# One fused retention and feed-forward kernel: the hand-written step table up to block 2, in another order

## The chip, the cores and the metric

The kernel runs on one core of one Trainium2 chip. The measure is device time in microseconds of one execution, of which lower is better. Six engines matter here: TensorE (PE, with its weight loads shown as PEld), VectorE (DVE), ScalarE (ACT), GpSimd (POOL), SyncE (SP), and the DMA engines, whose transfers are issued by SP, POOL and, at the start and the end, ACT. Each engine carries out its own instructions in the order in which they stand in the program; between engines only semaphores set an order.

## The reference: what is computed

Two layers, one after the other. The first is a retention layer (attention without softmax, with a decay per head) on q, k, v of 8 batches, 8 heads, 576 positions and 64 channels:

```
scores = (q @ k^T) / sqrt(64)
ret    = scores * gamma[h] ** (i - j)      for j <= i, else 0
x      = ret @ v                           heads side by side: 4608 tokens x 512
```

The second is a feed-forward layer on the 4608 tokens, with a snake activation, w_in of 512 x 2048, w_out of 2048 x 512 and one alpha for each of the 2048 columns:

```
h   = x @ w_in
g   = h + sin(alpha * h) ** 2 / (alpha + 1e-9)
out = g @ w_out
```

Inputs and output are float32; the kernel computes in float16 with float32 sums.

## The kernel before, in words

**Blocks.** The 512 first positions of each of the 8 batches make blocks 0 to 7 of 512 tokens; the 64 last positions of all batches make block 8. A block's x must be there before its feed-forward part, so attention for batch n+1 is done beside the feed-forward part of block n.

**Attention of one batch.** k and q come in halves of 256 positions (p = 0, 1), are scaled by powers of the decay and cast to float16 (step C, line 215, or line 210 on ACT), and are transposed, on PE for batches 0 and 1 and the first half of batch 2 (TR, copied out of PSUM by TK) or by a transposing DMA (CR). SP gives scores in PSUM, SM multiplies them by the causal mask (line 393; SO first copies them to float16), OU sums k times v over chunks of 128 positions, and FS, FA, NS and TS carry the state from chunk to chunk (FA and NS on two engines in turn: fade, then add; TS writes the state in float16, line 346). VA (line 462) adds masked scores times v to the output bank, ST (line 488) adds q times the state; XT copies the finished x to SBUF.

**Feed-forward part of one block.** GEMM1 has 16 units of four 512-column matmuls (line 584; G1 or H1 in the table). Each unit is followed by a sine on ACT (SI, line 593), a square (SQ, on ACT line 602, on DVE or POOL line 604) and a product that adds h (PR, on DVE, line 609), which writes gT and frees the PSUM bank. For the first four pairs of units of block 0 this is done in half blocks of 256 tokens (H1, HS, HQ, HP; lines 1067, 1079, 1094). GEMM2 has for each of four groups of 128 tokens four parts of four matmuls (line 623); part r reads gT of units 4r to 4r+3. The finished group is copied out of PSUM (line 633, or step OS) and stored by SP.

**What sets the order.** The steps up to block 2's start stand in a table, TABLE, one line a step, and the engine is often its last letter (V, A, G). follow() carries out the table line by line; as the scheduling is manual, an engine's queue holds its instructions in that order. Step LV n p loads v (POOL's queue), WI g and WO g load a quarter of w_in and w_out (POOL's queue), LK b nm p loads half of q or k (SP's queue; a last word names a load that it waits for), KB n m issues n filler matmuls of m columns, which write a PSUM bank that nobody reads. Behind the table a loop over blocks 2 to 8 takes over: each turn does one GEMM1 unit, then what todo lists for that unit (attention of the next batch at units 0, 4, 8 or so), the square, the product and one GEMM2 part from a list, `second`, which holds the parts of blocks 1 to 8 in order. Step GN in the table takes one part from the same list ahead of the loop. Where a part is the last of its group (`last`), the square and the product come after it:

```
second = [(n, u) for n in range(1, NBLK) for u in range(12 if n == NBLK - 1 else 16)]
...
    last = second[0][1] % 4 == 3
    if not last:
        square(n, u, A_); product(n, u)
    next_second()
    if last:
        square(n, u, A_); product(n, u)
while second:
    next_second()
```

What is still in the list after the loop is done at the end, followed by the last group in two halves (line 1228).

PSUM banks come from three pools: hp (three banks), op (one) and mm (two pairs); a step that takes a bank waits until the last reader of its former use is done. Raw q and k share six buffers.

Of the kernel before, what the change touches and what calls it, by code (L numbers as in the profile page):

```python
# [16 lines left out]
def kernel(  # L17
# [630 lines left out]
TR 0 0 k 1  # L648
LV 0 0
TR 0 0 q 1  # L650
KB 2 512 op
LV 0 1
WI 0
LK 0 k 1
LA
NO 0 0
TK 0 0 q AV
TK 0 0 k AV
SP 0 0 1
SP 0 0 0  # L660
AL
SO 0 0 0
AC
LP 0 q 1 0
LP 0 q 1 1
C 0 k 1 0 G
KB 2 512 op
C 0 k 1 1 G
TR 0 1 k 1
KB 2 512 hp  # L670
TK 0 1 k AA
C 0 q 1 1 G
WI 1
# [7 lines left out]
VA 0 0 1  # L681
FS 0
FA 0 0 V 1
TS 0 0 V
ST 0 0
NS 0 1
FA 0 1 G
OU 0 1 1
TS 0 1 V
NS 0 2  # L690
TS 0 2 G
AO
WI 2
TK 0 1 q AA
SP 0 1 0
SM 0 1 0
XT 0 0 AA
SP 0 1 1
SM 0 1 1
H1 0 1 0 op  # L700
HS 0 1 0
H1 0 0 0 hp
FA 0 2 G
NS 0 3
HS 0 0 0
HQ 0 0 0 V
HP 0 0 0
HQ 0 1 0 G
ST 0 1
VA 0 1 1  # L710
VA 0 1 0
H1 0 2 0 hp
XT 0 1 A
WO 0
WO 1
LK 1 q 0 w_in2
LK 1 k 0
LK 1 q 1 w_in2
LK 1 k 1 w_in2
HP 0 1 0  # L720
H1 0 3 0 mm
H1 0 0 1 mm
# [2 lines left out]
HP 0 2 0  # L725
HS 0 3 0
HQ 0 3 0 V
TS 0 3 G
HS 0 0 1
HQ 0 0 1 A  # L730
H1 0 1 1 op
H1 0 2 1 hp
H1 0 3 1 hp
G1 0 8 hp
HP 0 0 1
HP 0 3 0
# [12 lines left out]
HQ 0 2 1 G
HP 0 2 1  # L750
SQ 0 8 G
PR 0 8
HP 0 3 1
SQ 0 9 G
SQ 0 10 A
PR 0 10
PR 0 9
G1 0 12 hp
SI 0 11
SI 0 12  # L760
# [11 lines left out]
SQ 0 15 A  # L772
SQ 0 14 G
PR 0 13
C 1 q 0 1 V
PR 0 15
G2 0 0 0 op
G2 0 0 1 op
LV 1 0
G2 0 1 0 hp  # L780
G2 0 3 0 hp
G2 0 1 1 hp
PR 0 14
LV 1 1
C 1 q 0 0 G
WO 2
LK 2 q 0 w_out2
C 1 k 0 0 A
C 1 k 0 1 A
TR 1 0 q  # L790
LV 2 0
TR 1 0 k
G2 0 2 0 hp
TK 1 0 k A
LK 2 k 0 w_in0
LK 2 k 1 w_in1
LK 2 q 1 w_in1
C 1 k 1 1 V
TK 1 0 q V
SP 1 0 1  # L800
SP 1 0 0
G2 0 3 1 hp
SO 1 0 1
C 1 k 1 0 V
SO 1 0 0
C 1 q 1 1 G
C 1 q 1 0 G
# [5 lines left out]
G2 0 2 1 hp
TK 1 1 k A
SP 1 1 0
SM 1 0 1
OU 1 0
# [35 lines left out]
C 2 k 0 1 V
FA 1 2 G
NS 1 3
C 2 q 0 0 V
# [97 lines left out]
VA 2 1 0
SI 1 13
C 3 k 1 0 G
SQ 1 13 A
PR 1 13
PR 1 10
G1 1 14 hp  # L960
# [12 lines left out]
PR 1 15
C 3 q 1 0 G
LV 3 0
TS 2 3 G
CR 3 1
GN 1
"""

    HALVES = [(0, "k"), (0, "q"), (1, "k"), (1, "q")]
# [1 line left out]
    V, A_, G_ = nc.vector, nc.scalar, nc.gpsimd  # L983

    with tc.manual_schedule():
# [174 lines left out]
        for n in range(2, NBLK):  # L1160
            A = A2
# [104 lines left out]
```

## Time and profile before

| | |
|---|---|
| time, median of 3 runs | 308.93 us (308.0 to 310.65) |
| the profiled execution's own time | 308.69 us |
| its span, first to last instruction | 306.7 us |
| TensorE busy | 296.4 us, 97% of the span |
| ScalarE busy | 227.0 us, 74% |
| VectorE busy | 191.6 us, 62% |
| GpSimd busy | 135.2 us, 44% |
| HBM read and written | 36.91 MB and 9.44 MB |
| granted TensorE clock | 1.00 |

The profile is of one execution; its own time is 2 us more than its span, for what lies before the first and behind the last instruction. Timelines list for each row the start, the time that the row spans, engine, line, operation, what is written and read, shapes and count; in brackets stands how long the engine was idle before and what ended that. A single 512-column matmul is shown with 0.38 us since its end is modelled, but such matmuls start 0.216 us after one another; four of them (a unit or a part) take 0.865 us of TensorE.

### The profile page before, as it was taken

How to read it: one execution, taken by the hardware profiler on the slowest of the kernel's cores; microseconds unless marked ns; L12 is line 12 of the kernel's file. 1: busy time of each engine (PE TensorE's matmuls, PEld its weight loads, DVE VectorE, ACT ScalarE, POOL GpSimd, SP SyncE). 2: the span in 40 equal slices, each digit the busy share in tenths (PEclk: the TensorE clock that was granted, in tenths of full speed). 3: DMA queues.
4: the chain of work that ended last, by engine and by line, in shares of the span. 5: the costliest groups of instructions: out<-in, count | busy, mean ns of one | idle time of the engine just before them, and what ended most of it. 6: DMA issues, size and time to landing. Idle time of an engine off the chain costs nothing.

```text
span 306.7 us, 7628 instructions
## 1 busy us (share of the span) xinstructions
PE 296.4 (97%) x3134; PEld 152.8 (50%) x3134; DVE 191.6 (62%) x266; ACT 227.0 (74%) x378; POOL 135.2 (44%) x158
## 2 busy tenths in 40 slices
PE   8789999999999999999999999999999999999994
PEld 7476445544444444544454445544544444444444
DVE  2878958799565357946997699546665333444401
ACT  1579873999688887788778878787877888888810
POOL 3887664869949839703960297219000000000000
PEclk9999999999999999999999999999999999999999
DMA  7999999997999787999899989984331111122133
GB/s 212 218 195 204 262 185 246 248 250 128 167 177 227 129 210 183 155 177 221 175 161 196 172 214 165 151 138 76 71 68 37 35 34 36 36 54 47 36 68 68
DMA packets 118017, 44.74 MB, mean 146 GB/s; under 512 B 84432, under 2 KB 113504, under 8 KB 117984
## 3 DMA queue, kind: packets, MB, share of 16 engines
q1 hardware_dynamic: 83792, 35.08, 56.5%
q0 software_dynamic: 33600, 8.92, 30.0%
q8 instruction: 24, 0.39, 0.5%
q10 hardware_dynamic: 592, 0.28, 0.4%
q14 instruction: 9, 0.07, 0.1%
HBM read 36.91 MB, written 9.44 MB: 151 GB/s over the span
## 4 chain that ended last, share of the span: by engine, by line
PE 79%; DMA 6%; DVE 5%; POOL 5%; ACT 2%; issue 2%; POOLq 0%; DVEq 0%; ACTq 0%
PE ops L623 36%; PE hps L584 33%; DMA w_in<-in_moe_w_in_dram 3%; DMA w_out<-in_moe_w_out_dram 3%; DVE gT L609 2%; PE o L462 2%; PE o L488 2%; PE hps L1067 2%; POOL v L128 1%; POOL q L215 1%; PE ops L1228 1%; DVE ret L393 1%; POOL ss_t L604 1%; ACT s_t L593 1%; PE kv L312 1%
## 5 line engine op out<-in xcount | busy, mean ns | idle before, releaser
L609 DVE SCALAR_TENSOR_TENSOR gT<-ss_t,inva,hps 128x512 f16<-128x512 f16 x136 | 100.4, 744 | 80.3 <-ACT ss_t L602 79.9
L623 PE MATMUL ops<-w_out,gT 128*128 128x512 f16 x560 | 140.9, 379 | 0.5 <-DMA w_out<-in_moe_w_out_dram 0.5
L584 PE MATMUL hps<-x,w_in 128*128 128x512 f16 x480 | 120.9, 379 | 1.0 <-DVE gT L609 0.6
L593 ACT ACTIVATE s_t<-hps,alpha_t 128x512 f16<-128x512 f32 x136 | 92.9, 685 | 33.1 <-PE hps L584 31.7
L584 PEld LDWEIGHTS <-w_in 128*128 128x128 f16 x544 | 53.0, 98 | 64.5 <-issue 1.6
L623 PEld LDWEIGHTS <-gT 128*128 128x128 f16 x560 | 53.0, 98 | 61.2 <-issue 0.7
L602 ACT ACTIVATE ss_t<-s_t 128x512 f16<-128x512 f16 x127 | 79.9, 631 | 2.7
L346 POOL TENSOR_TENSOR s<-kvs,cn 128x512 f16<-128x512 f32 x28 | 30.6, 1093 | 57.0 <-ACT kvs L319 50.1
L633 ACT COPY osb<-ops 128x512 f32<-128x512 f32 x31 | 18.2, 586 | 11.7 <-PE ops L623 11.7
L126 POOL DMA_DIRECT2D v<-in_v_dram x32 | 22.0, 728 | 0.0
L393 DVE TENSOR_TENSOR ret<-sc,mask 128x1024 f16<-128x1024 f32 x12 | 14.4, 1215 | 4.6 <-PE sc L376 4.6
L215 DVE TENSOR_TENSOR q<-q,cn 128x512 f16<-128x512 f32 x17 | 14.1, 854 | 4.3 <-DMA q<-in_q_dram 4.3
L584 PE MATMUL hps<-x_rest,w_in 128*128 128x512 f16 x64 | 16.4, 379 | 0.0
L215 POOL TENSOR_TENSOR q<-q,cn 128x512 f16<-128x512 f32 x14 | 15.5, 1120 | 0.1
L432 DVE TENSOR_TENSOR ret<-sc,two 128x1024 f16<-128x1024 f32 x12 | 14.6, 1218 | 0.0
L604 POOL TENSOR_TENSOR ss_t<-s_t 128x512 f16<-128x512 f16 x10 | 10.5, 1059 | 6.6 <-ACT s_t L593 5.0
L236 ACT CAST x<-o 128x1024 f16<-128x1024 f32 (+1 forms) x13 | 10.8, 851 | 3.1 <-PE o L488 2.7
L359 POOL TENSOR_TENSOR kvs<-s,kvs 128x256 f32<-128x256 f32 x15 | 11.5, 769 | 1.2
L358 POOL TENSOR_TENSOR s<-kvs,cn 128x256 f32<-128x256 f32 x15 | 11.0, 731 | 0.0
L462 PE MATMUL o<-ret,v 64*64 64x128 f16 (+1 forms) x512 | 9.4, 213 | 0.6 <-DVE ret L393 0.6
L215 POOL TENSOR_TENSOR k<-k,cn 128x512 f16<-128x512 f32 x9 | 9.9, 1106 | 0.4 <-DMA k<-in_k_dram 0.4
L215 DVE TENSOR_TENSOR k<-k,ct 128x512 f16<-128x512 f32 x12 | 10.0, 830 | 0.0
(74 smaller groups left out, 209.0 us busy)
## 6 DMA issues: line engine op xcount, KB each, us to landing
out_dram<-osb SPq DMA_DIRECT2D x70, 128.0 KB, 3.3
q<-in_q_dram SPq DMA_DIRECT2D x14, 512.0 KB, 7.5
k<-in_k_dram SPq DMA_DIRECT2D x32, 128.0 KB, 5.1
k<-in_k_dram SPq DMA_DIRECT2D x7, 512.0 KB, 7.1
q<-in_q_dram SPq DMA_DIRECT2D x8, 256.0 KB, 5.3
v<-in_v_dram POOLq DMA_DIRECT2D x8, 256.0 KB, 6.0
w_in<-in_moe_w_in_dram POOLq DMA_DIRECT2D x4, 512.0 KB, 8.1
w_out<-in_moe_w_out_dram POOLq DMA_DIRECT2D x4, 512.0 KB, 7.8
```

The costliest lines, as they stand in the source:

```text
L126: nc.gpsimd.dma_start(t_[halves(g), :, s], v[b, :, xs, :].rearrange("h i d -> i h d"))
L215: eng.tensor_tensor(half[b, nm, p][:, :, :, t, :], raw[b, nm, p].rearrange("p (a t) (r d) -> p a t r d", t=2, r=2)[:, :, t], (ct if nm == ...
L346: (eng or nc.gpsimd).tensor_tensor(d_, self.kvs[:, n].unsqueeze(2).to_broadcast([P, 4, 2, D]), g2.unsqueeze(3).to_broadcast([P, 4, 2, D]), ...
L393: nc.vector.tensor_tensor(ret.rearrange("p t (z x) -> p (t z) x", z=2)[:, :, 0:n], sc.rearrange("p t (z x) -> p (t z) x", z=2)[:, :, 0:n], ...
L432: nc.vector.tensor_tensor(ret.rearrange("p t (a x) -> p (t a) x", a=n), sc.rearrange("p t (a x) -> p (t a) x", a=n), m_.unsqueeze(1).to_br ...
L462: nc.tensor.matmul(o[g][halves(t), x0 : x0 + 128].rearrange("p (r i) -> p r i", r=2)[:, :, i0:], x, y, start=(t, g) not in begun, stop=las ...
L584: nc.tensor.matmul(hps, w_in16[:, a, fc * P : (fc + 1) * P], x_of[n][:, a], start=(a == 0), stop=(a == KT - 1),)
L593: nc.scalar.activation(s_t, hps, mybir.ActivationFunctionType.Sin, bias=0.0, scale=alpha_t[:, fc : fc + 1],)
L602: nc.scalar.activation(ss_t, s_t, mybir.ActivationFunctionType.Square)
L609: nc.vector.scalar_tensor_tensor(gT[n][:, fc, :], ss_t, inva[:, fc : fc + 1], hps, MULT, ADD)
L623: nc.tensor.matmul(ops[n, c], gT[n][:, fk, c * P : (c + 1) * P], w_out16[:, fk, :], start=(fk == 0), stop=(fk == FC - 1),)
L633: nc.scalar.copy(osb, ops.pop((n, c)))
```

## The change

Only TABLE is altered. It has one line less: of the three places with fillers between the first transposes and the first H1 (`KB 2` each) one is left, with `KB 3`; and a third GN has been added, so that three parts of block 1's GEMM2 stand ahead of the loop instead of two. All other lines are the same steps in another order, some on another engine. Line numbers behind the table are lower by one in the changed kernel. The diff, cut to what moves a wait, a load or an engine:

```diff
 TR 0 0 q 1
-KB 2 512 op
 LV 0 1
 WI 0
 LK 0 k 1
 LA
+LP 0 q 1 0
 NO 0 0
 TK 0 0 q AV
+LP 0 q 1 1
+C 0 k 1 1 G
+C 0 k 1 0 G
 TK 0 0 k AV
 SP 0 0 1
 SP 0 0 0
 AL
+KB 3 512 hp
+AC
 SO 0 0 0
-AC
-LP 0 q 1 0
-LP 0 q 1 1
-C 0 k 1 0 G
-KB 2 512 op
-C 0 k 1 1 G
 TR 0 1 k 1
-KB 2 512 hp
...
 FA 0 0 V 1
+NS 0 1
 TS 0 0 V
 ST 0 0
-NS 0 1
...
-TS 0 2 G
+WI 2
 AO
-WI 2
...
-FA 0 2 G
+FA 0 2 V
 NS 0 3
 HS 0 0 0
-HQ 0 0 0 V
+HQ 0 0 0 A
 HP 0 0 0
-HQ 0 1 0 G
+TS 0 2 G
...
+WO 1
 WO 0
-WO 1
+HQ 0 1 0 G
+TS 0 3 G
 LK 1 q 0 w_in2
-LK 1 k 0
+LK 1 k 0 w_in2
 LK 1 q 1 w_in2
-LK 1 k 1 w_in2
+LK 1 k 1 w_out1
...
 G1 0 11 op
+SI 0 11
 HQ 0 2 1 G
 HP 0 2 1
 SQ 0 8 G
-PR 0 8
 HP 0 3 1
 SQ 0 9 G
+PR 0 9
+PR 0 8
 SQ 0 10 A
 PR 0 10
-PR 0 9
...
+LV 1 1
+LV 1 0
 C 1 q 0 1 V
...
 WO 2
 LK 2 q 0 w_out2
+C 1 k 0 1 A
 C 1 k 0 0 A
-C 1 k 0 1 A
+C 1 q 0 0 G
 TR 1 0 q
-LV 2 0
+C 1 q 1 0 G
 TR 1 0 k
...
 SO 1 0 1
+SO 1 0 0
+C 1 q 1 1 V
+WO 3
+LV 2 0
 C 1 k 1 0 V
-SO 1 0 0
-C 1 q 1 1 G
-C 1 q 1 0 G
-WO 3
+TR 1 1 k
 TR 1 1 q
-TR 1 1 k
 TK 1 1 q V
+OU 1 0
+TK 1 1 k A
+G2 0 2 1 hp
+SP 1 1 0
...
-XT 1 0 VV
+FA 1 2 G
 TS 1 2 G
...
-XT 1 1 A
+XT 1 1 AA
+XT 1 0 V
+C 2 k 0 1 V
+C 2 q 0 0 V
+TR 2 0 q
...
 SQ 1 9 V
+C 3 q 0 0 G
+SQ 1 11 A
+PR 1 11
 PR 1 9
-PR 1 11
-C 3 q 0 1 G
-C 3 q 0 0 G
 TS 2 2 G
 C 3 k 0 1 G
+C 3 q 0 1 G
+C 3 q 1 1 G
 CR 3 0
 LV 3 1
-C 3 q 1 1 G
+C 3 k 1 0 G
 TS 2 1 G
...
+VA 2 1 1
 VA 2 1 0
...
 GN 0
-G1 1 15 mm
-VA 2 1 1
+GN 1
+G1 1 15 hp
 ST 2 1
...
-XT 2 1 AV
+XT 2 1 VV
 PR 1 15
 C 3 q 1 0 G
 LV 3 0
 TS 2 3 G
 CR 3 1
-GN 1
+GN 2
```

More of the change, by code (lines that the diff above doesn't have):

```diff
@@ L690 @@
 NS 0 2
-TS 0 2 G
+WI 2
 AO
-WI 2
 TK 0 1 q AA
+SP 0 1 1
 SP 0 1 0
@@ L697 @@
 XT 0 0 AA
-SP 0 1 1
 SM 0 1 1
@@ L702 @@
 H1 0 0 0 hp
-FA 0 2 G
+FA 0 2 V
 NS 0 3
 HS 0 0 0
-HQ 0 0 0 V
+HQ 0 0 0 A
 HP 0 0 0
-HQ 0 1 0 G
+TS 0 2 G
 ST 0 1
+VA 0 1 0
 VA 0 1 1
-VA 0 1 0
 H1 0 2 0 hp
 XT 0 1 A
+WO 1
 WO 0
-WO 1
+HQ 0 1 0 G
+TS 0 3 G
 LK 1 q 0 w_in2
-LK 1 k 0
+LK 1 k 0 w_in2
 LK 1 q 1 w_in2
-LK 1 k 1 w_in2
+LK 1 k 1 w_out1
 HP 0 1 0
@@ L727 @@
 HQ 0 3 0 V
-TS 0 3 G
 HS 0 0 1
@@ L732 @@
 H1 0 2 1 hp
-H1 0 3 1 hp
-G1 0 8 hp
 HP 0 0 1
@@ L740 @@
 HP 0 1 1
+H1 0 3 1 hp
 HS 0 3 1
 HQ 0 3 1 V
+G1 0 8 hp
 SI 0 8
@@ L751 @@
 SQ 0 8 G
-PR 0 8
 HP 0 3 1
 SQ 0 9 G
+PR 0 9
+PR 0 8
 SQ 0 10 A
 PR 0 10
-PR 0 9
 G1 0 12 hp
-SI 0 11
-SI 0 12
 SQ 0 11 V
@@ L764 @@
 PR 0 11
+SI 0 12
 SQ 0 12 V
@@ L774 @@
 PR 0 13
+PR 0 15
+LV 1 1
+LV 1 0
 C 1 q 0 1 V
-PR 0 15
 G2 0 0 0 op
 G2 0 0 1 op
-LV 1 0
 G2 0 1 0 hp
+G2 0 1 1 hp
 G2 0 3 0 hp
-G2 0 1 1 hp
 PR 0 14
-LV 1 1
-C 1 q 0 0 G
 WO 2
 LK 2 q 0 w_out2
+C 1 k 0 1 A
 C 1 k 0 0 A
-C 1 k 0 1 A
+C 1 q 0 0 G
 TR 1 0 q
-LV 2 0
+C 1 q 1 0 G
 TR 1 0 k
@@ L794 @@
 TK 1 0 k A
-LK 2 k 0 w_in0
-LK 2 k 1 w_in1
-LK 2 q 1 w_in1
+LK 2 k 0 v00
+LK 2 k 1 w_out1
+LK 2 q 1 w_in2
 C 1 k 1 1 V
@@ L803 @@
 SO 1 0 1
+SO 1 0 0
+C 1 q 1 1 V
+WO 3
+LV 2 0
 C 1 k 1 0 V
-SO 1 0 0
-C 1 q 1 1 G
-C 1 q 1 0 G
-WO 3
+TR 1 1 k
 TR 1 1 q
-TR 1 1 k
 TK 1 1 q V
-SM 1 0 0
[L813 to L817, printed above, removed]
+OU 1 0
+TK 1 1 k A
+G2 0 2 1 hp
+SP 1 1 0
+SO 1 1 0
+SM 1 0 1
+SM 1 0 0
 FS 1
 TS 1 0 G
+G2 0 3 2 hp
 G2 0 2 2 hp
-G2 0 3 2 hp
-SO 1 1 0
 SP 1 1 1
@@ L826 @@
 OU 1 1
-VA 1 0 1
 ST 1 0
 VA 1 0 0
+VA 1 0 1
+G2 0 1 2 hp
 G2 0 0 3 op
-FA 1 0 V
+FA 1 0 G
 NS 1 1
@@ L834 @@
 TS 1 1 V
-LV 2 1
-G2 0 1 2 hp
-G2 0 1 3 hp
 G2 0 2 3 hp
 C 2 q 0 1 A
+LV 2 1
+G2 0 1 3 hp
 OS 0 1 A
@@ L842 @@
 NS 1 2
-XT 1 0 VV
+FA 1 2 G
 TS 1 2 G
-VA 1 1 1
+ST 1 1
 SM 1 1 0
 VA 1 1 0
-ST 1 1
-XT 1 1 A
+VA 1 1 1
+XT 1 1 AA
[3 more added lines that the diff above has]
+TR 2 0 q
 OS 0 0 A
+NS 1 3
 C 2 k 0 0 V
 G2 0 3 3 hp
[L853 to L856, printed above, removed]
 TR 2 0 k
-TR 2 0 q
 TK 2 0 k A
@@ L861 @@
 SI 1 0
-OS 0 3 V
 TS 1 3 G
@@ L867 @@
 C 2 q 1 0 G
-CR 2 1
 G1 1 1 hp
+OS 0 3 V
 SI 1 1
-SQ 1 1 A
 TK 2 0 q V
@@ L874 @@
 SM 2 0 0
+SP 2 0 1
+SQ 1 1 A
+PR 1 1
 SQ 1 0 A
-PR 1 1
 PR 1 0
-SP 2 0 1
 SM 2 0 1
-LK 3 k 0 w_in2
-LK 3 q 0
+CR 2 1
+LK 3 k 0 v10
+LK 3 q 0 w_in0
 G1 1 2 hp
@@ L884 @@
 SQ 1 2 G
-LK 3 k 1 w_in0
-LK 3 q 1 w_out1
+LK 3 q 1
+LK 3 k 1 v20
 G1 1 3 op
@@ L890 @@
 OU 2 1
+SQ 1 3 A
 G1 1 4 hp
@@ L893 @@
 FS 2
-SQ 1 3 A
 FA 2 0 G
+PR 1 3
+NS 2 1
 PR 1 2
@@ L898 @@
 SQ 1 4 G
-NS 2 1
-PR 1 3
 FA 2 1 V
@@ L904 @@
 FA 2 2 G
+TS 2 0 V
 NS 2 3
-TS 2 0 V
 G1 1 6 mm
@@ L920 @@
 SI 1 7
+SI 1 9
 SQ 1 7 A
-SI 1 9
 SQ 1 8 G
@@ L926 @@
 G1 1 10 hp
+VA 2 0 1
+ST 2 0
+SP 2 1 1
+VA 2 0 0
 SI 1 10
-ST 2 0
-VA 2 0 1
-VA 2 0 0
+SQ 1 10 A
+PR 1 10
 XT 2 0 AA
-SP 2 1 1
 SM 2 1 1
 G1 1 11 op
-SQ 1 10 A
 SI 1 11
@@ L938 @@
 G1 1 13 mm
-SQ 1 11 A
+G1 1 14 hp
 SI 1 12
@@ L942 @@
 SQ 1 9 V
+C 3 q 0 0 G
+SQ 1 11 A
+PR 1 11
 PR 1 9
-PR 1 11
-C 3 q 0 1 G
-C 3 q 0 0 G
 TS 2 2 G
 C 3 k 0 1 G
+C 3 q 0 1 G
+C 3 q 1 1 G
 CR 3 0
 LV 3 1
-C 3 q 1 1 G
+C 3 k 1 0 G
 TS 2 1 G
 C 3 k 1 1 G
+SQ 1 12 A
+SI 1 13
+SQ 1 13 A
+VA 2 1 1
 VA 2 1 0
[L955 to L960, printed above, removed]
-GN 0
-G1 1 15 mm
-VA 2 1 1
+GN 0
+GN 1
+G1 1 15 hp
 ST 2 1
-SQ 1 12 A
 SI 1 14
@@ L969 @@
 PR 1 12
+PR 1 13
 PR 1 14
 SQ 1 15 A
-XT 2 1 AV
+XT 2 1 VV
 PR 1 15
```

## The prediction

> **What bounds the kernel now.** The page first: of a span of 306.7 us TensorE is busy for 296.4. The stage view says where the rest is; its columns are the stretch, its length, then busy us (and instructions) of PE, PEld, DVE, ACT, POOL, then granted clock and DMA.
>
> ```profile
> PE 296.4 (97%) x3134; PEld 152.8 (50%) x3134; DVE 191.6 (62%) x266; ACT 227.0 (74%) x378; POOL 135.2 (44%) x158
> ```
> ```profile
> 17.60:33.00 15.40, 15.28 (x137) 10.36 (x138) 13.51 (x28) 13.07 (x26) 10.66 (x12) 1.00 1.18 219
> 33.00:56.00 23.00, 22.00 (x319) 12.14 (x318) 17.19 (x27) 15.08 (x37) 15.07 (x16) 1.00 1.27 222
> 56.00:78.00 22.00, 21.13 (x280) 10.34 (x278) 19.40 (x28) 19.92 (x33) 19.09 (x20) 1.00 0.96 205
> 78.00:290.00 212.00, 212.00 (x2072) 102.44 (x2070) 130.04 (x165) 168.99 (x266) 79.16 (x97) 1.00 0.82 127
> ```
> From 78 to 290 us TensorE has no hole at all; from 17.6 to 78 it has small ones. Counted from start to start (a 512-column matmul follows the one before after 0.216 us, so four take 0.865), the excess over back-to-back work between 17.6 and 78 is 0.26 at 30.7, 0.05 at 32.7, 0.43 at 38.1, 0.31 at 39.3, 0.31 at 42.9, 0.41 at 48.6, then 0.19, 0.39, 0.30, 0.27 and 0.31 up to 76.7: 3.2 us in all. Ahead of 17.6 stand waits for loads: the waits list has 0.7 us of the first L1067 matmuls for w_in's first quarter. The changed order issues the same loads up to that quarter, in the same order and on the same queues, so this point stays, and **3.2 us is the most that any order behind it can gain**: the matmuls behind it are the same ones.
>
> **The change, part by part.**
>
> *Opening, to 17.6 us.* Three of six 512-column fillers go; alpha's copy (0.18 us on ACT) goes ahead of the 1.01 us score copy; NS 0 1 goes ahead of TS 0 0, which makes the state product on PE some 0.15 us late. All this lies in front of the 0.7 us wait for w_in and costs nothing while that wait lasts; without it, 0.15 us.
>
> *17.6 to 33 us.* One square (HQ 0 0 0) moves from DVE to ACT, where a row of such squares adds about 0.53 us each (24.20 to the next start at 24.73). ACT's copy of x (20.61 to 21.58) slips 0.36, to end at 21.95; its reader on PE starts at 22.24, so that is hidden by 0.3 us. ACT has no hole from there to 30 us, so the slip reaches POOL's run of four squares (25.69 to 29.91), which ends at 30.27. The product of unit 9, now first in its group, then starts at 30.3; three products at 0.66, a square at 0.45 and the product of unit 11 (0.75) end at 33.5. GEMM2's first group takes unit 11's bank; it started at 32.95 just as that product ended, and now starts at 33.5: **+0.57**. WI 2 is issued 2 us sooner (two steps of POOL now stand behind it), WO 1 and WO 0 1 us sooner; but the four w_in loads land at 17.58, 20.12, 22.69 and 25.38, back to back, so nothing lands sooner: 0. What SP waits for (w_in2, and now w_out1 for batch 1's last k) comes before SP's own turn at 30.38.
>
> *33 to 56 us.* The 0.57 meets a fixed point: the transposes of k wait for ACT's sixteen scalings, done at 38.49 either way, and C 1 q 0 0 is ready at 37.9, as it now stands behind WO 2 (0.8). They end at 38.9 instead of 38.6: +0.3. OU 1 0 (0.35) now stands between the transposes and SP 1 1 0, and hides the 0.31 wait for kT at 42.9: level at 46.2. Then comes the load of w_out's last quarter.
>
> ```profile
> 49.34 3.61 PE L623 MATMUL ops<-w_out,gT 128*128 128x512 f16 x16 [0.50 <-DMA w_out<-in_moe_w_out_dram]
> ```
> PE waits for it: issued at 41.17, it landed at 49.30. Now one cast fewer (1.28) and no v load (0.89) stand ahead of its issue on POOL: 38.9. If it keeps its 8.1 us it lands at 47.0; PE wants it at 49.56, as one more GEMM2 unit stands before it. The 0.41 goes, and so do 0.2 of small breaks, since VA's two halves run together. Bounds: a landing by its fastest neighbour (6.2 us) or its slowest (9.8) changes nothing, so 0.41 it is. Next late is C 2 q 0 0 on DVE, behind one copy of x instead of after two; I count 0.3 back. Block 1's first matmul starts at 55.42 for 55.67: **−0.25**.
>
> *56 to 78 us.* Unit 3's product goes ahead of unit 2's, which frees G1 7's bank (0.19 wait gone); other waits move by a tenth or two. By 73.1 PE is 0.4 ahead. But in this stage POOL is as full as PE, and its order decides the end of it. On POOL:
>
> ```profile
> 68.15 2.06 POOL L215 TENSOR_TENSOR q<-q,cn 128x512 f16<-128x512 f32 x2
> 70.16 1.04 POOL L346 TENSOR_TENSOR s<-kvs,cn 128x512 f16<-128x512 f32 x1
> 71.17 1.23 POOL L215 TENSOR_TENSOR k<-k,cn 128x512 f16<-128x512 f32 x1
> 72.34 0.94 POOL L128 DMA_DIRECT2D v<-in_v_dram  x1
> 73.30 1.06 POOL L215 TENSOR_TENSOR q<-q,cn 128x512 f16<-128x512 f32 x1
> 74.31 1.04 POOL L346 TENSOR_TENSOR s<-kvs,cn 128x512 f16<-128x512 f32 x1
> ```
> and on PE, in the same stretch:
>
> ```profile
> 74.31 1.02 PE L584 MATMUL hps<-x,w_in 128*128 128x512 f16 x4
> 75.27 0.42 PE L462 MATMUL o<-ret,v 64*64 64x128 f16 x16
> 75.62 0.62 PE L488 MATMUL o<-qT,s 128*128 128x128 f16 x8
> 76.07 1.03 PE L623 MATMUL ops<-w_out,gT 128*128 128x512 f16 x4
> 77.25 1.02 PE L584 MATMUL hps<-x,w_in 128*128 128x512 f16 x4
> ```
> The L488 matmuls (ST 2 1) need the state of the last POOL row (TS 2 1, ended 75.35). This POOL run starts when batch 3's first q lands, at 68.08. The new order puts one more cast ahead of TS 2 1: from 68.1, four q/k casts at 1.0, TS 2 2, the v load and one k cast of 1.0, then TS 2 1, give 76.3. PE gets to ST 2 1 at about 75.8 and waits till 76.4. Then x of block 2: the copy was split over DVE (76.27) and ACT (76.63 to 77.20); now both halves stand on DVE, 0.65 behind ST 2 1 and then 0.69 and 0.59 (the page's rate for two such casts, 1.28). Block 2's first matmul starts 1.98 behind ST 2 1: 78.4. One GEMM2 unit more (GN) is done by then, worth 0.865; against 77.25 + 0.865 = 78.11 the net is **+0.28**. Bounds: if the POOL run comes half a us sooner, −0.2; if it is slowed by one cast of 2.0 for two, +1.3.
>
> *78 us to the end.* GEMM2 now runs three units behind the loop's start, not two: each GEMM2 part stands one place nearer to the products that it reads. The tail shows the price. All engines, 288.7 to 293:
>
> ```profile
> 288.77 1.03 PE L584 MATMUL hps<-x_rest,w_in 128*128 128x512 f16 x4
> ...
> 289.63 3.64 PE L623 MATMUL ops<-w_out,gT 128*128 128x512 f16 x16
> 289.83 0.69 ACT L593 ACTIVATE s_t<-hps,alpha_t 128x512 f16<-128x512 f32 x1 [0.24 <-PE hps L584]
> 290.55 0.63 ACT L602 ACTIVATE ss_t<-s_t 128x512 f16<-128x512 f16 x1
> 291.22 0.75 DVE L609 SCALAR_TENSOR_TENSOR gT<-ss_t,inva,hps 128x512 f16<-128x512 f16 x1 [0.84 <-ACT ss_t L602]
> 292.02 0.98 PEld L623 LDWEIGHTS <-gT 128*128 128x128 f16 x6 [0.34 <-DVE gT L609]
> ```
> Behind the last GEMM1 unit come sine, square and product, 289.63 to 291.96, with nothing queued before them. The matmul that reads the product is the last of GEMM2's fourth part: two whole units (1.73) and three matmuls (0.65) stand ahead of it, 2.38 us, so it starts at 292.02 with no loss. With one unit (it has been run earlier) only 1.51 us stand ahead, and PE waits the difference: **+0.87**. In the loop GEMM1's next unit stands between as well, 2.38 us again: 0 to 0.02 a block. The copy of each output moves from units 1, 5, 9, 13 to 0, 4, 8, 12, beside the attention work; there the product of unit 0 comes at 113.9 instead of 113.3, and the bank is wanted at 115.0: covered by 1.1 us.
>
> **Sum.** −0.25 at 56 us is overwritten by the POOL run: +0.28 at block 2's start, +0.87 in the tail: **+1.15 us** on the profiled execution's 308.69, 309.8; the median shown (308.93) stands 0.24 above that run, so 310.0, and I say **309.9**: 0.3% slower, inside the 1% that a measurement of this kernel can tell from no change.
>
> **Rivals.**
>
> *The clock falls shut (slower).* Place: 9 to 17.6 us. With three fillers out, PE's pause before VA 0 0 0 grows from 0.62 to 1.1 us, and the one before the first scores from 0.42 to about 0.9. Price: the 55 opening fillers take 6.02 us, 0.107 each from start to start, while the 128-column transposes at 7.39 follow each other at 0.055: it took 6 us of work at half speed to open the clock. If it shut before 17.6, up to 6 us of matmuls would run at half speed, +3.0: 308.93 + 1.15 + 3.0 = 313.1. It decides once a pause reaches whatever length shuts the clock; the longest pause seen in the trace at full speed is 0.7, the new one 1.1, and half the stretch stays busy. The Trainium skill's TensorE: Matmul & The Clock Gate, in Part 1, puts that length at an idle window of about 3.4 us; by that rule this rival cannot happen, and no run here shows a pause so long. Chance 0.06.
>
> *The late copies cost in every block (slower).* If the covers of 1.1 us at units 0, 4 and 8 are wrong by what a 1 us copy adds, three waits of 0.3 in blocks 3 to 6 give 3.6: 313.7. Against: in the trace no such wait exists with the copy one unit later. Chance 0.12.
>
> *The front keeps its gain.* The POOL run is early, and most of the 3.2 us go: between 308.93 − 3.2 + 0.87 = 306.6 and 309.2. It needs batch 3's q to land well before 68; SP issues it behind eight output stores as before. Chance 0.20.
>
> *The tail's unit is no loss*, because something sets the end other than the product chain: 309.2. Nothing speaks for it; it lies in the forecast's range.
>
> **How the numbers follow.** Forecast (+0.3 to +2.3) 0.62; front keeps its gain 0.20, of which 0.04 are over 1% faster (305.8 or less, more than the floor of stalls allows, so only by drift); the two slower rivals 0.18, most of them over 1%; of the forecast 0.02 spills over. Faster 0.04, same 0.78, slower 0.18. The range leaves out about one in ten on each side: 307.3 to 312.6.
>
> **What would show it.** Right: the stretch up to 17.6 unchanged; GEMM2 opening at 33.5; no DMA wait near 49; a wait of L488 for POOL near 76 and of L584 for DVE's x near 78; a hole of 0.9 us in L623 behind the last GEMM1 unit, closed by DVE gT L609. Wrong: holes between 80 and 285 us, matmuls at half speed behind 17.6, a w_in landing later than 17.6, or a tail without the hole.

## The result and the profile after

The changed kernel takes **310.54 us** (median of 22 executions, 309.28 to 311.61) and the kernel before 309.15 us (22 executions, 308.0 to 310.65). The ratio is 1.0043, with a 95% interval of 1.0029 to 1.0057: 1.33 us slower, between 0.9 and 1.8, which lies within the 1% of no change. The profiled execution of the changed kernel took 309.28 us, with a span of 307.3 us.

The page's first line and the stage view of the changed kernel, in the columns of the view shown for the kernel before (stretch, length, busy us and instructions of PE, PEld, DVE, ACT and POOL, granted clock, DMA share, GB/s):

```profile
PE 295.4 (96%) x3131; PEld 152.2 (50%) x3131; DVE 189.7 (62%) x266; ACT 226.6 (74%) x379; POOL 133.8 (44%) x157
```
```profile
17.60:33.00 15.40, 15.15 (x132) 9.76 (x131) 14.24 (x29) 14.09 (x29) 9.17 (x10) 1.00 1.22 241
33.00:56.00 23.00, 21.61 (x318) 12.05 (x317) 15.82 (x25) 14.62 (x37) 14.91 (x17) 1.00 1.28 218
56.00:78.00 22.00, 20.97 (x280) 10.24 (x279) 19.55 (x29) 18.95 (x32) 18.89 (x20) 1.00 0.93 197
78.00:290.00 212.00, 212.00 (x2071) 102.33 (x2070) 126.46 (x165) 168.80 (x265) 78.75 (x96) 1.00 0.83 126
```

The long middle is as full as before. One thing must be put right ahead of any other reading: in this execution all first loads landed about 1 us sooner, w_in's first quarter at 16.46 us and not at 17.58, and the first expert matmul began at 16.55 and not at 17.62. Nothing shows that this is the change: in the profiles of the experiments below it begins at 16.62 to 18.16 with the opening of the kernel before, and at 16.72 to 17.71 with the changed one. So the two profiles are compared from the first expert matmul on:

| from the first expert matmul (us) | before | after | difference |
|---|---|---|---|
| GEMM2 opens | 15.33 | 15.59 | +0.26 |
| block 1's first G1 matmul | 38.05 | 38.55 | +0.50 |
| block 2's first G1 matmul | 59.62 | 60.97 | +1.35, of which 0.865 is a GEMM2 unit done sooner: +0.49 |
| from there to the last G1 matmul of all | 212.2 | 212.5 | +0.3 |
| from there to PE's last matmul | 13.12 | 13.12 | 0, with one unit (0.865) less to do: +0.87 |

The sum is 1.65 us in this pair of profiles, against 1.33 by the ratio. Two executions of one order differ as well. Block 1's first G1 matmul comes 38.55, 38.54, 38.11 and 39.79 us behind the first expert matmul in the changed kernel, e9, e10 and e1 of the experiments below, which share the order up to there, and 38.05, 37.88 and 38.73 in the kernel before, e8 and e2. So a row of the first two is good to some tenths at best, and only what several traces repeat can be called a property of the order. Three places carry the sum.

First, the POOL run and block 2's start. POOL, then PE, then DVE of the changed kernel, between 66 and 78 us (start, length, engine, line, operation; in brackets the idle time before and what ended it):

```profile
66.26 1.05 POOL L215 TENSOR_TENSOR k<-k,cn 128x512 f16<-128x512 f32 x1
67.27 1.05 POOL L215 TENSOR_TENSOR q<-q,cn 128x512 f16<-128x512 f32 x1
...
73.42 1.06 POOL L215 TENSOR_TENSOR k<-k,cn 128x512 f16<-128x512 f32 x1
74.42 1.04 POOL L346 TENSOR_TENSOR s<-kvs,cn 128x512 f16<-128x512 f32 x1
```
```profile
74.28 1.03 PE L584 MATMUL hps<-x,w_in 128*128 128x512 f16 x4
75.53 0.62 PE L488 MATMUL o<-qT,s 128*128 128x128 f16 x8 [0.22 <-POOL s L346]
75.98 1.03 PE L623 MATMUL ops<-w_out,gT 128*128 128x512 f16 x4
77.53 1.02 PE L584 MATMUL hps<-x,w_in 128*128 128x512 f16 x4 [0.52 <-DVE x L237]
```
```profile
76.19 1.29 DVE L237 CAST x<-o 128x512 f16<-128x512 f32 x2 [0.85 <-PE o L488]
```

The state product on PE (L488, ST 2 1) stands right behind the end of POOL's L346, which has a cast more ahead of it than before. Counted from start to start it comes 0.38 us late; then the two casts of x stand one behind the other on DVE, and block 2's first matmul comes another 0.68 us late, where the kernel before lost 0.31. The row at 67.27 has no bracket: in this execution POOL did not have to wait for batch 3's q.

Second, the tail. All engines of the changed kernel behind the last GEMM1 unit:

```profile
290.21 1.67 PE L623 MATMUL ops<-w_out,gT 128*128 128x512 f16 x7
...
291.79 0.75 DVE L609 SCALAR_TENSOR_TENSOR gT<-ss_t,inva,hps 128x512 f16<-128x512 f16 x1 [0.98 <-ACT ss_t L602]
...
292.60 1.68 PE L623 MATMUL ops<-w_out,gT 128*128 128x512 f16 x7 [0.71 <-DVE gT L609]
```

Seven matmuls and then a pause for the last product: the hole that was forecast, 1.092 us from start to start where 0.216 is due, so 0.88 us lost.

Third, something that was not forecast, at the end of the front. PE and DVE near 53 us:

```profile
47.93 3.63 PE L623 MATMUL ops<-w_out,gT 128*128 128x512 f16 x16
...
53.35 0.61 PE L275 MATMUL tr<-ident,q 128*128 128x128 f16 x8 [0.77 <-DVE kvs L334]
```
```profile
51.67 0.69 DVE L215 TENSOR_TENSOR k<-k,cn 128x512 f16<-128x512 f32 x1 [0.74 <-DMA k<-in_k_dram]
52.28 0.68 DVE L215 TENSOR_TENSOR q<-q,cn 128x512 f16<-128x512 f32 x1
```

The wait for w_out is gone: the 16 GEMM2 matmuls at 47.93 have no bracket. But the transposes of batch 2's q (L275) now come early, ahead of a GEMM2 unit, and wait for the cast of q on DVE. That cast stands behind a cast of k, which waited for its load. The q had landed at 49.96. This costs 0.84 us, twice what w_out's earlier load gave back. The same wait stands in the traces of e1, e3, e7, e9 and e10 below, which share this order, with 0.40 to 1.56 us.

### The profile page after: what moved, and what is told of

The parts are those of the page before. It is cut to its first block, busy times and chain, and to the rows that moved or that the text cites. A ratio compares the mean times of both kernels' runs of the same rounds, so it can differ in the third digit from the quotient of the medians.

```text
span 307.3 us, 7622 instructions
## 1 busy us (share of the span) xinstructions
PE 295.4 (96%) x3131; PEld 152.2 (50%) x3131; DVE 189.7 (62%) x266; ACT 226.6 (74%) x379; POOL 133.8 (44%) x157
## 4 chain that ended last, share of the span: by engine, by line
PE 75%; DVE 9%; DMA 7%; POOL 5%; issue 1%; ACT 1%; SPq 0%; DVEq 0%; POOLq 0%; ACTq 0%
PE ops L623 34%; PE hps L584 32%; DMA k<-in_k_dram 4%; DMA w_out<-in_moe_w_out_dram 3%; DVE ret L393 2%; DVE gT L609 2%; POOL ss_t L604 2%; PE o L488 2%; PE o L462 1%; PE ops L1227 1%; POOL k L215 1%; PE kv L312 1%; DVE kvs L334 1%; PE sc L407 1%; POOL v L128 1%
## 5 line engine op out<-in xcount | busy, mean ns | idle before, releaser
L609 DVE SCALAR_TENSOR_TENSOR gT<-ss_t,inva,hps 128x512 f16<-128x512 f16 x136 | 100.5, 745 | 83.0 <-ACT ss_t L602 82.2
L584 PE MATMUL hps<-x,w_in 128*128 128x512 f16 x480 | 120.5, 379 | 0.7 <-DVE x L237 0.5
L584 PEld LDWEIGHTS <-w_in 128*128 128x128 f16 x544 | 53.0, 98 | 63.9 <-issue 1.1
L346 POOL TENSOR_TENSOR s<-kvs,cn 128x512 f16<-128x512 f32 x28 | 30.9, 1103 | 60.0 <-ACT kvs L319 50.9
L633 ACT COPY osb<-ops 128x512 f32<-128x512 f32 x31 | 18.2, 586 | 14.6 <-PE ops L623 14.6
L584 PE MATMUL hps<-x_rest,w_in 128*128 128x512 f16 x64 | 16.4, 379 | 0.0
L215 POOL TENSOR_TENSOR q<-q,cn 128x512 f16<-128x512 f32 x13 | 14.1, 1101 | 0.2 <-PE hps L584 0.2
L359 POOL TENSOR_TENSOR kvs<-s,kvs 128x256 f32<-128x256 f32 x15 | 12.5, 834 | 1.2
L237 DVE CAST x<-o 128x1024 f16<-128x1024 f32 (+1 forms) x7 | 7.4, 1070 | 4.8 <-PE o L488 4.8
L358 POOL TENSOR_TENSOR s<-kvs,cn 128x256 f32<-128x256 f32 x15 | 10.2, 682 | 0.0
L462 PEld LDWEIGHTS <-v 64*64 64x64 f16 x512 | 7.3, 107 | 5.1 <-issue 3.4
```

Of the source, the lines that this page charges most:

```text
L215: eng.tensor_tensor(half[b, nm, p][:, :, :, t, :], raw[b, nm, p].rearrange("p (a t) (r d) -> p a t r d", t=2, r=2)[:, :, t], (ct if nm == ...
L346: (eng or nc.gpsimd).tensor_tensor(d_, self.kvs[:, n].unsqueeze(2).to_broadcast([P, 4, 2, D]), g2.unsqueeze(3).to_broadcast([P, 4, 2, D]), ...
L462: nc.tensor.matmul(o[g][halves(t), x0 : x0 + 128].rearrange("p (r i) -> p r i", r=2)[:, :, i0:], x, y, start=(t, g) not in begun, stop=las ...
L584: nc.tensor.matmul(hps, w_in16[:, a, fc * P : (fc + 1) * P], x_of[n][:, a], start=(a == 0), stop=(a == KT - 1),)
L609: nc.vector.scalar_tensor_tensor(gT[n][:, fc, :], ss_t, inva[:, fc : fc + 1], hps, MULT, ADD)
L633: nc.scalar.copy(osb, ops.pop((n, c)))
```

## The experiments

Each kernel is one of the two with a few steps edited. Ratios are to the kernel before, timed beside it on the same chip, with 95% intervals; one per mille is 0.31 us. A difference from the changed kernel is that of the two ratios, its interval that of two independent ones. "After" is the changed kernel (1.0043).

### e1, the tail: swap the units behind the last GEMM1 unit

```diff
         second = [(n, u) for n in range(1, NBLK) for u in range(12 if n == NBLK - 1 else 16)]
+        at = second.index((NBLK - 1, 3))
+        second[at], second[at + 1] = second[at + 1], second[at]
```


> The changed kernel, with the two units of block 7's GEMM2 swapped that stand behind the last GEMM1 unit: the first part of the second output group (it reads products 0 to 3) comes ahead of the fourth part of the first group (it reads product 15). Theory (the chain sine, square, product of the last unit is longer than the one unit ahead of its reader): the 0.88 us excess at 291.5 in the L623 matmuls closes to 0.05 or less, and the time falls by 0.87, from 310.54 to 309.7, a ratio to the kernel before of 1.0015 (1.0000 to 1.0030). Rival (the end is set by the last output copies and stores): the hole closes but the span does not get shorter, ratio 1.0043.

Measured: ratio 1.0012 (0.9994 to 1.0029), 309.66 us. PE of this kernel in the tail:

```profile
290.81 1.03 PE L584 MATMUL hps<-x_rest,w_in 128*128 128x512 f16 x4
...
291.67 3.64 PE L623 MATMUL ops<-w_out,gT 128*128 128x512 f16 x16
```

Sixteen matmuls in 3.64 us, as in the kernel before, and no bracket: a unit that needs only early products gives sine, square and product the time they need. The times fell by 1.0 us (0.3 to 1.6), about the size of the hole, so nothing behind it sets the end in its place.

### e2, the tail: the third unit alone, in the kernel before

```diff
 CR 3 1
 GN 1
+GN 2
```


> The kernel before, with one more step GN at the end of the table and nothing else: GEMM2 runs three units behind the loop's start. Theory: the tail shows the same hole of 0.87 us behind the last GEMM1 unit; the added unit covers the wait of 0.31 for x ahead of block 2's first matmul; no hole between 80 and 290; in all +0.56, ratio 1.0018 (1.0005 to 1.0030). Rival one (the tail's unit is no loss): -0.31, ratio 0.9990. Rival two (output copies one unit earlier cost 0.3 in three places per block): +3.6 or more, ratio 1.012.

Measured: ratio 1.0014 (0.9994 to 1.0034), +0.43 us (−0.2 to +1.1) where +0.56 was expected; PE at block 2's start, and in the tail:

```profile
75.27 0.62 PE L488 MATMUL o<-qT,s 128*128 128x128 f16 x8
75.73 1.89 PE L623 MATMUL ops<-w_out,gT 128*128 128x512 f16 x8
77.46 1.03 PE L584 MATMUL hps<-x,w_in 128*128 128x512 f16 x4
...
290.30 1.68 PE L623 MATMUL ops<-w_out,gT 128*128 128x512 f16 x7
292.68 1.69 PE L623 MATMUL ops<-w_out,gT 128*128 128x512 f16 x7 [0.71 <-DVE gT L609]
```

The hole is the same to the hundredth, in a kernel that has nothing else of the change. Two units behind L488 cover the copy of x in full; the 0.31 us wait is gone. PE is busy for 212.00 of the 212 us from 78 to 290, so the copies of outputs that come one unit sooner cost no hole that this view shows: the rival that priced them at 3.6 us is out.

### e8, the tail: third unit and swap, in the kernel before

Both edits above at once.

> The kernel before, with a third GN at the table's end and the last block's two units swapped. Theory: the third unit covers the 0.31 wait for x at block 2's start and the swap takes away the tail's hole, so -0.31, ratio 0.999 (0.9975 to 1.0005); against the run with the third GN alone (1.0014) that is 0.87 us less. Rival (running three units ahead costs elsewhere in the loop, by small slips where a product comes late): ratio 1.000 to 1.002, with slips over 0.1 us in L623 matmuls between 80 and 290 us.

Measured: ratio 0.9997 (0.9978 to 1.0016). The hole is gone and block 2's start has no wait for x, yet only a part of the 0.31 shows, if any. The interval holds both theories. The traces say that running three units ahead is not quite free: blocks 3 to 5 take 30.93, 30.93 and 32.19 us in the kernel before, 31.00, 30.99 and 32.30 in the changed kernel, and 31.10, 30.93 and 32.29 here. That is 0.2 to 0.3 us in all, in slips too small to carry a bracket. The largest in this kernel is 0.17, ahead of the GEMM2 matmuls at 112.19. There ACT's copy of an output (L633, 111.55 to 112.14) had to follow the 1.01 us copy of kv (L319), and it ends 0.05 ahead of those matmuls; e2 shows the same at 207.12, also 0.17. This is the mechanism of the late copies, at a size that costs a tenth or two and not 3.6 us.

### e3, block 2's start: the state and the copy of x as before

```diff
-C 3 k 1 0 G
 TS 2 1 G
+C 3 k 1 0 G
...
-XT 2 1 VV
+XT 2 1 AV
```


> The changed kernel, with two steps at block 2's start as in the kernel before: the state TS 2 1 one cast sooner on POOL, and the copy of x split over DVE and ACT. Theory (the POOL run and the copy on one engine hold block 2's start): the wait of L488 for POOL (0.38 excess at 75.5) goes, the wait for x (0.68 excess at 77.5) falls to about 0.3; in all -0.75, 309.8, ratio 1.0020 (1.0005 to 1.0035). Rival (something else holds block 2's start, the products of block 1 or the cast that is now later): the excess moves elsewhere between 74 and 80, ratio 1.0043.

Measured: ratio 0.9998 (0.9981 to 1.0015), 1.4 us under the changed kernel (0.7 to 2.1), more than the 0.75 expected. In its trace L488 no longer waits, but the copy of x does not come sooner: 0.76 us of excess, as ACT's half stands behind a sine and a square (77.61 to 78.87). So in this trace the state is what was gained, and the split copy gave nothing.

### e9, block 2's start: the state alone

```diff
-C 3 k 1 0 G
 TS 2 1 G
+C 3 k 1 0 G
```


> The changed kernel, with TS 2 1 one cast sooner on POOL, and the copy of x left on DVE for both halves: half of what e3 did. Theory (the late state is the larger loss, as it grows with whatever PE has gained before it): the wait of L488 for POOL is under 0.1, and the ratio to the kernel before is 1.001 to 1.003, 0.4 to 1.0 us below the changed kernel. Rival (the copy of x on one engine is what costs): the wait moves from L488 to L584 and the ratio stays 1.0035 to 1.0045.

Measured: ratio 1.0013 (0.9995 to 1.0031), 0.9 us under the changed kernel (0.2 to 1.6). PE at block 2's start:

```profile
74.67 1.03 PE L584 MATMUL hps<-x,w_in 128*128 128x512 f16 x4
75.54 0.61 PE L488 MATMUL o<-qT,s 128*128 128x128 f16 x8
75.99 1.03 PE L623 MATMUL ops<-w_out,gT 128*128 128x512 f16 x4
77.53 1.02 PE L584 MATMUL hps<-x,w_in 128*128 128x512 f16 x4 [0.52 <-DVE x L237]
```

L488 follows L584 with no bracket, and the wait for x is what it was. So the cast ahead of TS 2 1 was what made the state late, and taking the state sooner is enough to win most of what e3 won. By the traces the state is worth 0.38 and the copy of x 0.37 (0.68 against 0.31 before), so which of them is the larger loss is not shown; the 0.9 of the medians has 0.38 in its interval.

### e4, the front: batch 2's q cast ahead of its k cast

```diff
-C 2 k 0 1 V
 C 2 q 0 0 V
+C 2 k 0 1 V
```


> The changed kernel, with DVE's cast of batch 2's first q ahead of that of its k: q has landed at 50.0 and k only at 51.6, and the transposes of q on PE wait for the cast behind it (0.84 excess at 52.4). Both theories say that this excess goes, so that block 1's first matmul comes 0.7 to 0.8 sooner, counted from the first expert matmul. Theory one, as in the prediction (POOL's run from 66 us on is held by the landing of batch 3's q, and overwrites what was gained): nothing is left at block 2's first matmul, ratio 1.0043 (1.0030 to 1.0055). Theory two (POOL's run follows PE's pace, by a square that waits for its sine): 0.5 to 0.8 reaches the end, ratio 1.0022 (1.0010 to 1.0030).

Measured: ratio 1.0042 (1.0023 to 1.0062): nothing. All but 0.07 of the 0.84 us excess at the transposes is gone. Yet block 1's first matmul does not come 0.7 to 0.8 sooner: it stands 38.50 us behind the first expert matmul, for 38.55 in the changed kernel. In this execution PE had lost as much ahead of the transposes, 0.46 more in the wait for POOL's cast of batch 1's q (37.8) and 0.24 at the VA matmuls (48.4). So this trace can't say what becomes of a gain. Further on, POOL and then PE of this kernel:

```profile
66.89 1.05 POOL L215 TENSOR_TENSOR k<-k,cn 128x512 f16<-128x512 f32 x1 [0.33 <-issue]
68.30 1.05 POOL L215 TENSOR_TENSOR q<-q,cn 128x512 f16<-128x512 f32 x1 [0.36 <-DMA q<-in_q_dram]
```
```profile
74.53 1.03 PE L584 MATMUL hps<-x,w_in 128*128 128x512 f16 x4
76.57 0.62 PE L488 MATMUL o<-qT,s 128*128 128x128 f16 x8 [1.00 <-POOL s L346]
```

Here batch 3's q is still on its way when POOL asks for it. Counted from the first expert matmul the cast of q starts at 51.44, for 50.72 in the changed kernel. L488 then waits 1.17 us where the changed kernel waited 0.38, and block 2 starts 0.73 later although block 1 started level. So the state is what holds L488, and a late landing of q is paid in full; whether the edit or the execution made it late is not shown.

### e5, the front: w_out's last quarter sooner, in the kernel before

```diff
 TR 1 0 q
-LV 2 0
 TR 1 0 k
...
 WO 3
+LV 2 0
```


> The kernel before, with one step moved: batch 2's first v load stands behind the load of w_out's last quarter, not ahead of it; that load is issued 0.9 us sooner. Both theories: the wait of L623 for w_out near 49 us (0.41 excess, 0.50 in the waits) is gone or under 0.15. Theory one (as in the prediction: POOL's run of casts, which begins when batch 3's q lands, overwrites what the front gains): nothing is left at block 2's first matmul, ratio to the kernel before 1.0000 (0.9988 to 1.0012). Theory two (the gain passes on to the end): -0.4, ratio 0.9987.

Measured: ratio 1.0000 (0.9979 to 1.0021). The GEMM2 matmuls that waited for w_out run through:

```profile
50.78 0.42 PE L462 MATMUL o<-ret,v 64*64 64x128 f16 x16
51.13 3.63 PE L623 MATMUL ops<-w_out,gT 128*128 128x512 f16 x16
```

The interval is too wide to exclude 0.4 us. In the trace the gain is lost again ahead of block 1 and not at the POOL run: from GEMM2's opening to block 1's first matmul pass 22.75 us, for 22.72 in the kernel before, as the scores (L376 at 42.23) now wait 0.62 for the copy of q where 0.24 was the wait for k's. The wait for w_out itself is not a fixed part of the order before: the matmuls at the same place of e2 and e8, which share that order, carry no bracket.

### e10, the front alone

The changed table up to `TK 2 0 k A`, just ahead of block 1's first expert matmul, and the table of the kernel before from there on.

> The changed order up to the copy of batch 2's first transposed k (just ahead of block 1's first expert matmul), and the order of the kernel before from there on: the front of the change alone. Theory one (what the front does is overwritten by POOL's run of casts): 0 to +0.3, ratio to the kernel before 1.000 to 1.001, and the change's loss stands in the part behind. Theory two (block 1 starts some 0.5 us later, and that reaches the end): +0.5 to +0.8, ratio 1.0016 to 1.0026.

Measured: ratio 1.0006 (0.9985 to 1.0027), and its trace reaches block 2's first matmul 59.97 us behind the first expert matmul, for 59.62 in the kernel before. The best estimate is +0.2 us, and −0.5 to +0.8 is possible, so theory two is not excluded by the time. In the trace block 1 starts at 38.11, level with the kernel before (38.05). The loss by the front is small if there is one; that POOL's run overwrote something can't be read from this run, as there was next to nothing to overwrite.

### e6, the clock: no fillers in the opening

```diff
 AL
-KB 3 512 hp
 AC
```


> The changed kernel without its three 512-column fillers of the opening (0.65 us of PE work; nothing of the result). So far 4 of 67 executions of the kernel before show a mean granted clock of 0.9955 or less (some 3.4 us at half clock near 10 to 14 us), and 15 of 80 of the seven kernels with the changed opening; in those the time is about 0.9 longer. Theory (emptier opening, clock falls shut more often): 6 or more of 12 executions are at 0.9955 or less, and the time is 0.3 to 1.0 above the changed kernel, ratio to the kernel before 1.005 to 1.008. Rival (it takes one long pause, and there is none): 0 to 4 of 12, ratio 1.0035 to 1.0050.

Measured: ratio 1.009 (1.0058 to 1.0122), from 6 executions, 311.23 us. All six have a mean granted clock between 0.987 and 0.992. Rows of the stage view of this kernel:

```profile
8.03:11.43 3.40, 1.60 (x43) 1.25 (x44) 2.16 (x5) 1.98 (x4) 3.36 (x5) 0.95 1.50 234
11.43:14.83 3.40, 2.89 (x64) 2.37 (x63) 2.91 (x5) 1.53 (x4) 2.34 (x4) 0.50 1.44 200
14.83:17.95 3.12, 3.12 (x90) 2.31 (x88) 2.58 (x6) 2.05 (x4) 2.31 (x3) 0.50 1.18 189
17.95:21.00 3.05, 3.05 (x59) 2.66 (x58) 3.05 (x3) 2.11 (x5) 3.02 (x4) 1.00 1.24 208
```

PE ran at half clock from 11.1 to 17.9 us. The fillers, which compute nothing, keep the clock open in most executions: 20 of 22 of the changed kernel are above 0.9955, and none of these six. By the ratios 0.65 us of them are worth about 1.5 us (0.4 to 2.5).

### e7, e11 and e12: several edits together

The first of three kernels has the tail's swap, both edits at block 2's start, and a second GEMM2 unit behind L488 in the changed kernel:

```diff
 GN 0
-GN 1
 G1 1 15 hp
 ST 2 1
+GN 1
```


> The changed kernel with four table edits: the last block's units swapped as in e1; TS 2 1 one cast sooner and the copy of x split as in e3; and the second GEMM2 unit of block 1 moved from ahead of the last GEMM1 unit of block 1 to behind ST 2 1, so that two units (1.73 us) cover the copy of x. Theory: the three holes of the changed kernel go (0.88 in the tail, 0.38 at ST 2 1, 0.68 at x), 310.54 - 1.9 = 308.6, ratio to the kernel before 0.998 (0.996 to 1.000). Rival (POOL's run holds ST 2 1 all the same, since PE now comes there 0.86 sooner): the wait for the state is 0.3 to 0.9 and the ratio 1.000 to 1.002.

Measured: ratio 1.0009 (0.9990 to 1.0028). The rival's wait came: the copy of x is covered, but PE reaches L488 0.86 us sooner and waits for the state, 0.96 us from start to start.

```profile
75.23 1.03 PE L584 MATMUL hps<-x,w_in 128*128 128x512 f16 x4
77.05 0.62 PE L488 MATMUL o<-qT,s 128*128 128x128 f16 x8 [0.80 <-POOL s L346]
77.51 1.89 PE L623 MATMUL ops<-w_out,gT 128*128 128x512 f16 x8
79.24 1.03 PE L584 MATMUL hps<-x,w_in 128*128 128x512 f16 x4
```

The second takes the state out of the run of casts, and has seven more fillers in the opening; it also has the edits of e7 and the cast order of e4:

```diff
 TR 0 0 q 1
+KB 4 512 op
...
 TR 0 1 k 1
+KB 3 512 hp
...
 TS 2 2 G
+TS 2 1 G
 C 3 k 0 1 G
```


> The changed kernel with the edits of e7, TS 2 1 moved further up on POOL (right behind TS 2 2, three casts and a v load sooner), the casts of batch 2 in the order of e4, and seven fillers more in two pauses of the opening. Theory (e7 was held by POOL alone, 0.96 us at ST 2 1, and a shut clock in 5 of its 12 executions): that wait goes, at most 1 of 12 executions has a clock of 0.9955 or less; 309.35 - 0.96 - 0.4 = 308.0, ratio to the kernel before 0.995 to 0.998. Rival (another wait takes its place, products of block 1 or x): ratio 0.999 to 1.001.

Measured: **ratio 0.9956** (0.9942 to 0.9970), 307.55 us, faster than both kernels. Its PE between 73 and 79 us:

```profile
73.36 1.03 PE L584 MATMUL hps<-x,w_in 128*128 128x512 f16 x4
74.22 0.61 PE L488 MATMUL o<-qT,s 128*128 128x128 f16 x8
74.67 1.89 PE L623 MATMUL ops<-w_out,gT 128*128 128x512 f16 x8
76.40 1.03 PE L584 MATMUL hps<-x,w_in 128*128 128x512 f16 x4
```

There is no bracket left here. None of its 12 executions had a clock of 0.9955 or less. The runs do not separate what each of its edits gave.

The third does the like to the kernel before: third unit and swap, v load behind w_out's last quarter, TS 2 1 right behind TS 2 2.

> The kernel before with four edits: a third GN at the table's end and the last block's units swapped (e8), the v load behind w_out's last quarter (e5), and TS 2 1 right behind TS 2 2 on POOL. Theory (the 0.41 gained at w_out's load now passes POOL, as the state no longer stands behind its casts): -0.3 of e8 and -0.2 to -0.5 more, ratio 0.997 to 0.9985. Rival (the gain is lost on DVE or ACT between 49 and 76 us): as e8, 0.9990 to 1.0000.

Measured: ratio 0.9997 (0.9976 to 1.0018); the rival's number. In its trace neither w_out nor POOL holds PE, but a product (L609) does, 0.33 us at 74.8, and block 1 starts 39.31 us behind the first expert matmul, later than in any trace with this opening but one. In this execution the transposes of batch 1's k waited for ACT's scalings between 37.1 and 39.2, 1.6 us in all for 0.4 in the kernel before, so the 0.41 was outweighed long before the POOL run.

## Why the prediction was right

The time forecast was 309.9 with a range of 307.3 to 312.6, and the forecast's +1.15 us came as +1.33. The two terms that make the sum, block 2's start and the tail, came by the mechanisms forecast, and the wait for the state and the tail's hole were each removed by an edit of its own (e9, e1). The front was forecast with the wrong sign, and that it did not spoil the sum is in part luck. Step by step:

- **Opening.** "This point stays" held for the order of the loads, but 17.6 us was the landing of one execution; over the profiles the first expert matmul starts between 16.5 and 18.2. The few tenths of the steps compared are smaller than that, so they had to be counted from that matmul.
- **17.6 to 33 us.** +0.57 was forecast for GEMM2's opening; the traces with the changed opening and an open clock give 15.59 to 15.61, against 15.33 in the kernel before: +0.26 to +0.28. The term was mis-sized, and may be nil: the opening of the kernel before gives 15.44, 15.49 and 15.99 in e8, e12 and e2.
- **33 to 56 us.** Right for w_out (the wait gone, though e2 and e8 show that the 0.41 was no fixed part of the order before) and for the wait at 42.9 (gone). Wrong in the line "I count 0.3 back" for C 2 q 0 0: the transposes of q lost 0.84, so block 1 started +0.50 late, not −0.25. The step read the order of DVE's queue by its casts and not by what the cast ahead of it waits for, batch 2's k, which lands 1.6 us behind q.
- **"Overwritten by the POOL run".** Half right. What PE gains just ahead of L488 is taken by the state: in e7 PE came 0.86 sooner and waited 0.96. But the run does not always start on the landing of batch 3's q, as the forecast had it. In e3, e4, e7, e9 and e10 its first cast of q waits for that landing, 0.34 to 0.36; in the changed kernel and e1 it follows the work ahead of it without a pause. There a loss passes through: block 1 of e1 starts 1.24 us later than that of the changed kernel, and block 2 1.25 later. So neither the front's gains nor its losses can be called void. In the pair compared, block 1 stood 0.75 later than forecast and L488 only 0.19, which is why the wrong sign did little harm there; in e1's execution L488 came 1.44 later than forecast.
- **Block 2's start.** +0.28 forecast, +0.49 in the trace, of which +0.11 stands at L488 and +0.37 at the copy of x. L488 was put at 76.4, on a clock on which the first expert matmul starts 1.07 us later: 75.33 here, against a measured 75.53. The 1.98 us from there to block 2's first matmul measured 2.00.
- **78 us to the end.** The tail's +0.87 measured 0.88, closed by the swap and made again by the third unit alone. "0 to 0.02 a block" was too small for blocks 3 to 5, which took 0.06 to 0.11 more each.

The rivals. *The late copies*: refuted at the price of 3.6 us, as there is no hole between 78 and 290 us; slips of up to 0.17 by this mechanism stand in e2 and e8. *The front keeps its gain*: not borne out, as the front gained nothing (+0.50 in the pair, a ratio of 1.0006 for the front alone). *The tail's unit is no loss*: refuted. *The clock falls shut*: neither as forecast nor absent. The execution profiled for e3, with the changed kernel's opening, shows it:

```profile
7.05:10.45 3.40, 1.70 (x39) 1.19 (x36) 1.76 (x4) 1.07 (x2) 3.11 (x4) 0.99 1.33 273
10.45:13.85 3.40, 3.40 (x68) 2.16 (x60) 3.23 (x3) 1.37 (x3) 3.40 (x4) 0.51 1.63 193
13.85:17.25 3.40, 2.14 (x104) 1.70 (x98) 2.21 (x5) 2.89 (x7) 2.25 (x4) 1.00 1.21 180
```

Half clock for 3.4 us, then open again. Taking a mean granted clock of 0.9955 or less as the sign of it, it came in 17 of 92 executions of the seven kernels with the changed opening (the changed kernel, e1, e3, e4, e7, e9, e10), and in 5 of 144 of those with the opening of the kernel before (96 of that kernel itself, and e2, e5, e8, e12). Within a kernel such executions are longer by 1.2 us on average (weighted by how many there were). So it is more frequent with the changed opening by about 15 in 100, which would be worth 0.15 × 1.2 = 0.2 us of the mean. But the share varies from 0 of 10 (e4) to 5 of 12 (e7), and of the 22 executions behind the 1.33 only 2 show it, 0.24 us longer than the rest; of the 1.33 itself the clock explains next to nothing. The price of 3.0 was too high for these executions, because the clock came back by itself after 3.4 us (e3 and e7), which at half speed can cost no more than 1.7; without the fillers it stayed shut for 6.8. The condition ("once a pause reaches whatever length shuts the clock") was wrong in kind, as the next section but one shows.

## What to carry to other kernels

When the bound engine takes one instruction out of another engine's run of work (here the state out of POOL's casts), move that instruction ahead of the work that it need not wait for, before polishing anything in front of it: e9 won 0.9 us (0.2 to 1.6) by one step. What leads such a run can change from one execution to the next, a landing in one and the bound engine's own pace in another; look at several traces before calling a gain in front of it lost. A unit of work pulled forward to fill one hole is missing from the place it came from; look whether it covered a dependent chain there, and whether an independent unit can take its place. Before two profiles are compared to tenths of a microsecond, count both from the first matmul behind the first loads.

## What the runs showed of the hardware

**What shut the clock was a thin window, not a long pause.** In every trace the granted clock changes only at steps of 3.41 us, counted from where it first opens, which is 4.1 to 7.1 us into the span. So the openings can be cut into such windows. Up to 24 us the 14 traces have 76 of them at full clock. Behind four of these the clock fell to half, and they are the four in which PE was least busy; four of the least busy of the other 72 stand below them:

| trace | window, us | PE busy, of 3.41 us | longest pause in it | clock in the next window |
|---|---|---|---|---|
| e7 | 6.54 to 9.95 | 1.68 | 0.85 | half |
| e3 | 6.97 to 10.38 | 1.71 | 0.85 | half |
| e6 | 7.70 to 11.11 | 1.72 | 0.85 | half |
| e5 | 15.06 to 18.47 | 1.77 | 1.64 | half |
| e5 | 4.82 to 8.23 | 1.95 | 1.21 | full |
| e6 | 4.29 to 7.70 | 2.02 | 1.39 | full |
| e10 | 12.01 to 15.42 | 2.07 | 1.16 | full |
| changed kernel | 5.93 to 9.34 | 2.08 | 0.85 | full |

Pauses of 1.2 to 1.4 us left the clock open and pauses of 0.85 did not save it, so the length of a pause does not decide. In these openings the border lies between 1.77 and 1.95 us of PE work in a window. As the windows begin elsewhere in each execution, the same order can fall on either side of it, and fillers lift a window that would be too thin. The busy time of PE is not the whole of the measure: in the last microseconds of e3 a window with 1.42 us of 256-column matmuls (L1227) was followed by full clock. The Trainium skill's TensorE: Matmul & The Clock Gate, in Part 1, has a free-running window of about 3.4 us, and the throttled state after at least one idle window. The length and the free run agree with the windows above, and with the 6.8 us, two windows, of the kernel without fillers; "idle" does not, as PE was half busy.

**A steadier kernel.** The 12 executions of e11 lie within 0.9 us (307.28 to 308.19); those of every other kernel with 10 or more span 2.1 to 3.4 us. No experiment separates the seven fillers from the other edits of that kernel, so what narrows it is open.
